# New places for all side jobs of a kernel generation, and a new order of its ring buffers, in a fused adaLN, S4 convolution and bilinear FFN kernel

## The chip, the cores and the metric

The kernel runs on one core of one Trainium2 chip. The metric is the device time in microseconds (us) of one execution; the times of a kernel are given as the median of its runs. A profiled execution is one further execution, seen instruction by instruction; its span runs from the first to the last instruction that the profile shows.

## What is computed

The inputs are a sequence `A_u` of 2048 rows of 640 channels, a condition vector `c`, and the weights. Cut to what matters:

```python
mod = (silu(c) @ w_mod).reshape(1, 6, 1, -1)          # sa, ca, ga, sb, cb, gb
h = layernorm(x) * (1 + ca) + sa
# S4: P[d,n,l] = exp(dt[d] * A[d,n] * l);  K[d,l] = Re sum_n C[d,n] P[d,n,l] dt[d] B[d,n]
y = irfft(rfft(pad(h)) * rfft(pad(K)))[:2048] + h * Dskip
x = x + ga * y
h = layernorm(x) * (1 + cb) + sb
x = x + gb * (((h @ w_gate) * (h @ w_up)) @ w_down)    # 640 -> 1536 -> 640
```

Length is 2048, there are 640 channels (five groups `db` of 128), 192 complex states per channel, and a hidden width of 1536. The time index l is split, so that exp(dt A l) is a product of short tables: tables are made, and their products are formed on the fly and multiplied on TensorE.

## The kernel before, in words

The program has two parts. The first generates the convolution kernel K and, beside that, does everything that the convolution needs; the second is the bilinear FFN, a long run of matmuls (L1059 and L1463) that the change leaves alone.

**The generation.** There are 40 blocks n (8 per channel group), each of three sub-steps, in the loop `for t in range(3*NK+24)`. A block passes through four engines. POOL (`kg_pool`, all at L710) forms three outer sums or products ahead of use: Ph (the angles of the next block), EQ and EP. ACT (L230) turns angles into sines, into PSUM tiles `tra` and `trb`. DVE multiplies the two: QtA and QtB (L765 to L767), PtA (L772), PtB (L792). PE contracts QtA with PtA (`kg_ma`, L807) and QtB with PtB (`kg_mb`, L822). EQ, EP, Ph, PtA and `tr` have two buffers each, so POOL forms EQ of block n+2 only after DVE's last QtB instruction (L767) of block n. Twice per channel group POOL also makes tables, `tab_ph` (L649, L650, L674, L693 to L695) and `tab_eq` (L674, L704, L705).

**The side jobs.** Everything else of the first part is cut into phases of Python generators, which `at` files under numbers and `due` lets go:

```python
        for v in ts:
            jobs.setdefault(v // 10, []).append((v, it))
...
        for _, g in sorted(jobs.pop(x, []), key=lambda j: j[0]):
            next(g, None)
```

In the loop, `due(2*t)` stands ahead of DVE's products of the sub-step and `due(2*t+1)` behind them and ahead of POOL's and PE's pieces. A block so has six steps; steps 0 to 239 lie in the generation, those below 0 ahead of it, and those from 240 on behind it. Within its engine each phase stands where its number puts it; engines take their instructions strictly in this order and wait by semaphores. The row of numbers is the dict `SCHED`. The jobs it places are:

- `mod_l`, `u_modr` (L360), `u_fold`, `u_modc`, `u_modg`: loads of `w_mod`, the six modulation rows, their folding.
- `u_stats`, `row_stats`, `u_hm`: loads of the rows of x, their layernorm, and its store to DRAM.
- `u_seeds(db)` (key `q`), 14 segments for each channel group after the first: loads, DVE arithmetic (L579 to L619, L644), and functions of ACT from three table sets, from which the tables of POOL come. The last segment (L644, L645) is what `tab_ph` of that group waits for.
- `e0`: ACT's exponentials for the second half of the first group, seven of LP, one of RH and one of RL, between two table loads.
- `u_k`, `u_pre`, `u_g`, `u_c` (L889; six adds on DVE, L930 to L936; inverse L946; store of WD), `u_d` (load TV from WD, matmul L967, add L971 or L974): the Fourier stages of K, of h and of their product.
- `rows`, `raw`, `split_g`, `u_head` (transposes L1139, matmuls L1176), `warm` (L1149; 30 and 4 matmuls into a tile that nobody reads): the beginning of the second part, at steps from 244 on.

**The buffers.** `ring(pool, shape, name)` gives a new tile the next letter of the string `SLOT[name]`, which decides the buffer, and so which earlier user it has to wait for:

```python
    def ring(pool, shape, name, dtype=F32):
        return pool.tile(shape, dtype, name=name + next(slot[name]), bufs=1)
```

The rings are the PSUM tiles psfa to psfc of the side jobs, and tiles in SBUF: gh, hf, TV, xs, Kt, W and f16.

Of the kernel before, what the change touches and what calls it, by code (L numbers as in the profile page):

```python
# [31 lines left out]
    ml=(-885, -929, -989),  # L32
    mr=(((98, 154), (90, 130)), ((-884, 78), (-877, 73)), ((-885, -881), (-889, 132))),
    st=(
        (-955, 11),
        (-929, 195),
        (-874, 149),
        (-925, 128),
        (-938, 121),
        (-879, 152),  # L40
        (-869, 167),
        (-924, 162),
        (-995, -925),
        (-938, -871),
        (-885, 93),
        (-990, -871),
        (50, 180),
        (51, 214),
        (-930, -878),
        (-927, 39),  # L50
    ),
    hm=(
        (120, 388),
        (119, 390),
        (123, 234),
        (-949, 306),
        (-1000, 254),
        (112, 246),
        (231, 293),
        (-871, 309),  # L60
        (266, 333),
        (324, 384),
        (315, 372),
        (134, 256),
        (463, 511),
        (335, 429),
        (391, 541),
        (479, 545),
    ),
    rstd=(228, 229),  # L70
    tab=(487, 829),
    fo=(157, 189, 197, 222),
    e0=(138,),
    ds=(205, 222, 503, 397),
    mc=((-872, 289, 307, 356, 356), (217, 378, 439, 446, 461), (309, 570, 620)),
    q=(
# [4 lines left out]
    ),  # L81
    pre=(
# [5 lines left out]
    ),  # L88
    c=(
# [56 lines left out]
    w=(2508, 2575, 2790, 2776, 2819, 2829),  # L146
# [1505 lines left out]
```

## Time and profile before

| what | value |
|---|---|
| median of 3 runs | 1003.26 us (1000.94 to 1003.36) |
| profiled execution, own time | 1001.29 us |
| its span | 999.2 us, so 2.09 us lie around it |
| TensorE clock granted, mean | 0.961 |
| busy: PE, DVE, POOL, ACT | 900.0, 762.8, 564.3, 561.9 us |
| generation on POOL | from 27.7 to 433.5 us |
| end of the first part on PE | 518.5 us |

The profile lists busy time by engine, groups of instructions with what ended the idle time before them, and the chain of work that ended last. In a group such as `EQ<-LQ,RH` the names are the tiles written and read; the line is that of the kernel or of a helper (L230 is the helper that records every ACT function, so there one goes by the tiles). A timeline row gives start, duration, engine, line, and in brackets the idle time before it with what ended that.

### The profile page before, as it was taken

The page shows a single profiled execution, that of the slowest core. Times are in us where ns is not written, and L with a number is a line of the kernel's source. Part 1 is how long each engine was busy: PE and PEld are TensorE (multiplying, and loading weights), DVE is VectorE, ACT ScalarE, POOL GpSimd, SP SyncE. Part 2 cuts the span into 40 slices and gives each one's busy share as a digit, 9 for nine tenths or more (in the row PEclk, how much of TensorE's full clock was granted, in tenths as well). Part 3 has the DMA queues.
Part 4 walks back from the last instruction along what each step waited for, and adds up shares of the span by engine and source line. Part 5 has one row for each costly group of instructions (what it writes and reads, how often), then busy time and mean ns, then how long its engine had stood idle before and what let it go on. Part 6 is the DMA issues. An engine that isn't in the chain of part 4 may idle for free.

```text
span 999.2 us, 26832 instructions
## 1 busy us (share of the span) xinstructions
PE 900.0 (90%) x11192; PEld 727.2 (73%) x11192; DVE 762.8 (76%) x1399; ACT 561.9 (56%) x1048; POOL 564.3 (56%) x415
## 2 busy tenths in 40 slices
PE   4867898899789689998888999999999999999998
PEld 3565556675576467776555888879998888889998
DVE  8798569889979997975769788777576887768452
ACT  4869989987878979752354323235463422223331
POOL 5978899799789899930032667650112365542000
PEclk9877889999899899999999999999999999999999
DMA  8728754555256454577673442535635232212341
GB/s 265 254 50 301 227 176 135 194 163 167 68 163 202 129 161 120 164 248 214 210 210 123 153 150 87 184 132 159 209 134 202 88 105 80 79 53 59 100 159 53
DMA packets 147817, 153.16 MB, mean 153 GB/s; under 512 B 9200, under 2 KB 125424, under 8 KB 146288
## 3 DMA queue, kind: packets, MB, share of 16 engines
q1 hardware_dynamic: 145968, 148.43, 46.8%
q10 hardware_dynamic: 1728, 3.02, 0.8%
q8 instruction: 88, 1.44, 0.6%
q14 instruction: 33, 0.27, 0.1%
HBM read 110.45 MB, written 40.96 MB: 152 GB/s over the span
## 4 chain that ended last, share of the span: by engine, by line
PE 63%; DVE 16%; ACT 10%; issue 4%; DMA 4%; POOL 2%; SPq 1%; DVEq 0%; ACTq 0%; POOLq 0%
PE pa L1059 26%; PE pa L1463 16%; PE kg L807 2%; DMA xsb<-A_u 2%; PE kg L822 2%; PE psfc L889 2%; ACT L230 1%; PE psfb L889 1%; PE psfa L889 1%; PE psfc L946 1%; PE psfb L946 1%; PE psfa L946 1%; PE psfc L868 1%; ACT trb L230 1%; PE psfa L844 1%
## 5 line engine op out<-in xcount | busy, mean ns | idle before, releaser
L710 POOL TENSOR_TENSOR EQ<-LQ,RH 128x1536 f32<-128x1536 f32 x40 | 124.2, 3105 | 9.9 <-DVE QtB L767 9.7
L230 ACT ACTIVATE z<-pa 128x512 f32<-128x512 f32 x24 | 14.4, 598 | 175.7 <-POOL a L1430 112.1
L1024 DVE TENSOR_TENSOR wsgl<-wga,wsgh 128x640 fp32r<-128x640 f32 x72 | 70.0, 976 | 46.1 <-ACT wsgh L230 46.1
L1412 POOL TENSOR_TENSOR z<-z,s 128x512 f32<-128x512 f32 x24 | 32.1, 1337 | 126.5 <-DVE s L1411 72.0
L230 ACT ACTIVATE wsgh<-wga 128x640 fp32r<-128x640 f32 x72 | 52.5, 732 | 65.1 <-PE pa L1463 47.9
L1024 DVE TENSOR_TENSOR wtl<-tf,wth 128x256 fp32r<-128x256 f32 (+1 forms) x72 | 42.7, 594 | 48.3 <-ACT wth L230 48.3
L1463 PE MATMUL pa<-wsgh,sh 128*128 128x384 f32 (+1 forms) x304 | 69.4, 309 | 0.0
L1463 PE MATMUL pa<-wsgh,sl 128*128 128x384 f32 (+1 forms) x304 | 69.0, 308 | 0.0
L1463 PE MATMUL pa<-wsgl,sh 128*128 128x384 f32 (+1 forms) x304 | 69.0, 308 | 0.0
L710 POOL TENSOR_TENSOR Phb<-LH,DH 128x1536 int32<-128x1536 int32 x20 | 62.3, 3115 | 11.2 <-ACT tra L230 11.2
L710 POOL TENSOR_TENSOR EP<-LP,RH 128x768 f32<-128x768 f32 x40 | 66.1, 1651 | 0.0
L710 POOL TENSOR_TENSOR Pha<-LH,DH 128x1536 int32<-128x1536 int32 (+1 forms) x21 | 62.5, 2974 | 2.2 <-ACT trb L230 1.9
L1036 POOL TENSOR_TENSOR tf<-wur,wgb 128x256 f32<-128x256 f32 x23 | 17.8, 776 | 75.6 <-DVE wtl L1024 50.0
L822 PE MATMUL kg<-QtB,PtB 64*32 64x64 f32 x2560 | 48.7, 229 | 5.4 <-DVE QtB L766 5.3
L822 PEld LDWEIGHTS kg<-QtB,PtB 64*32 64x32 f32 x2560 | 41.6, 114 | 15.4 <-issue 6.5
L1463 PEld LDWEIGHTS pa<-wsgh,sl 128*128 128x128 f32 x304 | 46.4, 187 | 0.0
L1463 PEld LDWEIGHTS pa<-wsgl,sh 128*128 128x128 f32 x304 | 46.3, 187 | 0.0
L1059 PE MATMUL pa<-sh,wtl 128*128 128x512 f32 x144 | 45.0, 394 | 1.4 <-DVE wtl L1024 1.2
L1463 PEld LDWEIGHTS pa<-wsgh,sh 128*128 128x128 f32 x304 | 46.3, 187 | 0.0
L1059 PE MATMUL pa<-sh,wth 128*128 128x512 f32 x144 | 44.9, 393 | 0.5 <-ACT wth L230 0.5
L1059 PE MATMUL pa<-sl,wth 128*128 128x512 f32 x144 | 44.5, 390 | 0.0
L1430 POOL TENSOR_TENSOR a<-s,z 128x512 f32<-128x512 f32 x24 | 38.8, 1618 | 5.4 <-DVE s L1429 5.4
(604 smaller groups left out, 2925.2 us busy)
## 6 DMA issues: line engine op xcount, KB each, us to landing
wga<-wdg SPq DMA_DIRECT2D x24, 640.0 KB, 5.0
wga<-B_w_gate SPq DMA_DIRECT2D x12, 640.0 KB, 5.9
wgb<-B_w_gate SPq DMA_DIRECT2D x24, 320.0 KB, 3.4
wur<-B_w_up SPq DMA_DIRECT2D x24, 320.0 KB, 4.0
xb<-x2d SPq DMA_DIRECT2D x6, 1280.0 KB, 5.7
TVb<-WD SPq DMA_DIRECT2D x22, 256.0 KB, 3.6
t_tw<-w_mod SPq DMA_DIRECT2D x3, 1600.0 KB, 8.5
t_ti<-w_mod SPq DMA_DIRECT2D x3, 1600.0 KB, 7.9
```

What stands on the lines that cost most here:

```text
L230: return S.activation(o, i, f, **kw)
L710: G.tensor_tensor(o.rearrange("p x (h l) -> p x h l", l=8), lo.unsqueeze(2).to_broadcast([P, rows, nh, 8]), hi.rearrange("p h x -> p x h") ...
L807: PE.matmul(kg[j * 32 : j * 32 + 32, dd, :], PtA[:, c, dl * 4 + j, :], QtA[:, c, dl * 4 + j, :], start=dd == 0 and c == 0, stop=False, til ...
L822: PE.matmul(kg[j * 32 : j * 32 + 32, dd, :], PtB[lo : lo + 64, c, r, :], QtB[lo : lo + 64, c, r, :], start=False, stop=dd == 7 and c == 1, ...
L889: PE.matmul(r[c][par * 64 : par * 64 + 64, i, :], t_tw[:, k0 + k, c, :], src[:, k, :], start=True, stop=True, tile_position=(0, par * 64))
L946: PE.matmul(r[par][:, i], t_ti[lo : lo + 64, qd * 4 + i, c, :], x[lo : lo + 64, c, i, :], start=c == 0, stop=c == 1, tile_position=(lo, 0))
L1024: V.tensor_tensor(lo, v, hi, op=OP.subtract)
L1036: E.tensor_tensor(t[:, 0:2], u[:, 0:2], g[:, 0:2], op=OP.subtract)
L1059: PE.matmul(ps, w[a][:, k], x[b][:, l], start=n == 0 and m == 0, stop=n == 2 and m == len(ks) - 1)
L1412: G.tensor_tensor(ZT[i], ZT[i], S67[i], op=OP.add)
L1430: G.tensor_tensor(a_tile(NF + i % NF), c, ZT.pop(i), op=OP.mult)
L1463: PE.matmul(ACC[tb][t][c], x[:, ts], w[:, cs], start=st, stop=f == NF - 1 and n == 2 and (c == 0 or t % 2 == 1))
```

## The change

Only numbers and letters change: the entries of `SCHED` and the strings in `SLOT`. Each engine executes the same instructions, but for ACT, which has 26 table loads in place of 24: a load is put in wherever a function needs another set than the one before it in ACT's order. The file gets five lines longer, so that a line of before stands five lines lower after the change.

```diff
 SCHED = dict(
-    ml=(-885, -929, -989),
-    mr=(((98, 154), (90, 130)), ((-884, 78), (-877, 73)), ((-885, -881), (-889, 132))),
+    ml=(-880, -938, -960),
+    mr=(((144, 184), (129, 179)), ((-877, 76), (-871, 133)), ((-890, -867), (-887, 14))),
...
-    rstd=(228, 229),
+    rstd=(180, 188),
...
-    e0=(138,),
+    e0=(29,),
...
-        (989, 1089, 1237, 1248, 1250, 1264, 1295, 1295, 1327, 1332, 1349, 1349, 1350, 1366),
+        (992, 1022, 1107, 1268, 1278, 1287, 1296, 1299, 1300, 1307, 1317, 1317, 1319, 1324),
...
-    w=(2508, 2575, 2790, 2776, 2819, 2829),
-    wl=(2444, 2450),
-    wm=(2801, 2834),
-    h=(2480, 2716, 2875, 2876, 2878, 2878, 2878, 2878),
+    w=(2574, 2477, 2623, 2825, 2760, 2598),
+    wl=(2501, 2487),
+    wm=(2775, 2703),
+    h=(2718, 2774, 2804, 2819, 2853, 2861, 2863, 2869),
```

The strings of the rings Ph, PtA, tr, W and f16 stay as they are; Kt, TV, gh, hf, psf and xs get others of the same length. What this does to the order of an engine is shown at three places.

**ACT, first blocks.** These are rows of before around `e0`, in block 2: two evictions of modulation rows (TVa, TVb), a table load, the exponentials, a load back, and the sines of the next sub-step.

```order
L230 ACTIVATE trb<-PtAa 128x512
L230 ACTIVATE TVa<-psfc 1x256
L230 ACTIVATE TVb<-psfb 1x256
L230 ACT_TABLE_LOAD
L230 ACTIVATE LP_146<-RL_156 128x96 x7
L230 ACTIVATE RH_153<-RH_153 128x1056
L230 ACTIVATE RL_156<-RL_156 128x288
L230 ACT_TABLE_LOAD
L230 ACTIVATE tra<-Pha 128x512
```

After the change the same rows stand in block 0, right behind the second pair of sines of that block:

```order
L235 ACTIVATE trb<-ab 128x512
L235 ACTIVATE TVb<-psfa 1x256
L235 ACTIVATE ab<-Pha 128x512
L235 ACTIVATE tra<-Pha 128x512
L235 ACTIVATE tra<-ab 128x512
L235 ACT_TABLE_LOAD
L235 ACTIVATE LP_146<-RL_156 128x96 x7
L235 ACTIVATE RH_153<-RH_153 128x1056
L235 ACTIVATE RL_156<-RL_156 128x288
L235 ACTIVATE ab<-Pha 128x512
L235 ACT_TABLE_LOAD
L235 ACTIVATE trb<-Pha 128x512
```

The exponentials and their two loads have moved by eleven steps, ahead of the last sines of block 0 (`trb<-Pha`, which POOL's third Ph waits for).

**DVE, the seeds of the fourth channel group.** Rows of before in block 22, between QtB of block 21 and PtAa of block 22: QtA of block 22, the six adds of `u_c`, and the first row of the segment with the reciprocal.

```order
L767 SCALAR_TENSOR_TENSOR QtB<-tra,EQ_141 128x8x32
L601 TENSOR_SCALAR psfb<-ptb 128x192
L765 TENSOR_TENSOR QtA<-trb,EQ_140 128x32x32
L766 TENSOR_TENSOR QtA<-trb,EQ_140 128x16x32
L767 SCALAR_TENSOR_TENSOR QtA<-trb,EQ_140 128x16x32
L930 TENSOR_TENSOR TVb<-psfc,ghb 128x512
L931 TENSOR_TENSOR TVb<-psfc,ghb 128x512
L932 TENSOR_TENSOR psfc<-psfa,ghb 128x512
L933 TENSOR_TENSOR psfa<-psfa,ghb 128x512
L935 TENSOR_TENSOR TVb<-TVb,psfc 128x512
L936 TENSOR_TENSOR TVb<-TVb,psfa 128x512
L614 SCALAR_TENSOR_TENSOR prm<-ptb,dt_98,psfb 128x192
```

After the change the reciprocal's segment stands right behind QtB of block 21, then the six adds, and from these on the row goes:

```order
L940 TENSOR_TENSOR TVa<-TVa,psfa 128x512
L941 TENSOR_TENSOR TVa<-TVa,psfb 128x512
L649 COPY RL_155<-psfc 128x96
L649 COPY RL_156<-psfc 128x96
L650 TENSOR_SCALAR ptb<-psfc 128x192
L770 TENSOR_TENSOR QtA<-trb,EQ_140 128x32x32
L771 TENSOR_TENSOR QtA<-trb,EQ_140 128x16x32
L772 SCALAR_TENSOR_TENSOR QtA<-trb,EQ_140 128x16x32
L777 TENSOR_TENSOR PtAa<-tra,EP_142 128x1024
```

The last segment of the seeds (L649, L650; before L644, L645) now stands ahead of QtA and PtAa of block 22; before it stood behind both.

**PE, the end of the first part.** Rows of before from the last pieces on: `u_d` (L967), the 34 warm matmuls (L1149), the transposes (L1139) and products (L1176) of the head.

```order
L967 MATMUL psfb<-TVb,ct 32x512 x4
L1149 MATMUL psg<-wsgh 128x512 x34
L967 MATMUL psfc<-TVa,ct 32x512 x4
L967 MATMUL psfa<-TVb,ct 32x512 x4
L1139 MATMUL psfb<-ident,hfa 128x128 x4
L1139 MATMUL psfc<-ident,hfb 128x128 x4
L967 MATMUL psfa<-TVa,ct 32x512 x4
L1139 MATMUL psfb<-ident,hfc 128x128 x4
L1176 MATMUL psg<-hh_6985,wsgh 128x512
```

After the change:

```order
L972 MATMUL psfa<-TVa,ct 32x512 x4
L1154 MATMUL psg<-wsgh 128x512 x30
L972 MATMUL psfb<-TVb,ct 32x512 x4
L972 MATMUL psfc<-TVa,ct 32x512 x4
L972 MATMUL psfa<-TVb,ct 32x512 x4
L1144 MATMUL psfb<-ident,hfc 128x128 x4
L1144 MATMUL psfc<-ident,hfa 128x128 x4
L972 MATMUL psfa<-TVa,ct 32x512 x4
L1144 MATMUL psfb<-ident,hfb 128x128 x4
L1181 MATMUL psg<-hh_7302,wsgh 128x512
```

Four of the warm matmuls have gone ahead of the last inverse; the third `u_d` behind the warm ones (of channel group 4, quarter 2) stands ahead of the head's first transposes, and a fourth follows (group 0, quarter 2). Before, that fourth one and the `u_d` of group 4, quarter 3, came as the very last pieces of the first part; after, the latter stands between two products of the head.

More of the change, by code (lines that the diff above doesn't have):

```diff
@@ new lines @@
+    hm=(
+        (350, 404),
+        (197, 446),
+        (63, 188),
+        (-948, 283),
+        (-866, 201),
+        (2, 196),
+        (193, 237),
+        (-895, 316),
+        (253, 338),
+        (338, 365),
+        (264, 341),
+        (38, 228),
+        (354, 517),
+        (365, 462),
+        (472, 540),
+        (517, 565),
+    ),
+    rstd=(180, 188),
+    tab=(644, 765),
+    fo=(200, 212, 246, 268),
+    e0=(29,),
+    ds=(386, 334, 572, 308),
+    mc=((-869, 234, 279, 323, 374), (225, 501, 521, 567, 581), (346, 429, 486)),
```

162 lines of the change are left out of this document (74 added, 88 removed), and 45 rows, old and new, of tables (c, d, g, pre).

## The prediction

> **What bounds the kernel now.** I read the page's totals first, then busy time by stretch, then the groups of the engine that paces the first part, then what it waits for. The totals, and the engines' shares of the chain that ended last:
>
> ```profile
> PE 900.0 (90%) x11192; PEld 727.2 (73%) x11192; DVE 762.8 (76%) x1399; ACT 561.9 (56%) x1048; POOL 564.3 (56%) x415
> PE 63%; DVE 16%; ACT 10%; issue 4%; DMA 4%; POOL 2%; SPq 1%; DVEq 0%; ACTq 0%; POOLq 0%
> ```
>
> PE looks like the bound everywhere, but that is an average over two parts. By stretch (columns: length, then busy us of PE, PEld, DVE, ACT and POOL with counts, the granted clock, DMA share, GB/s):
>
> ```profile
> 300.00:434.00 134.00, 116.08 (x2902) 86.59 (x2898) 119.85 (x195) 111.87 (x204) 128.41 (x74) 0.96 0.53 157
> 434.00:545.00 111.00, 94.36 (x1136) 67.34 (x1134) 78.90 (x190) 48.19 (x90) 10.68 (x16) 0.98 0.66 203
> 545.00:999.00 454.00, 446.74 (x2378) 395.27 (x2376) 316.82 (x506) 157.27 (x305) 169.35 (x152) 1.00 0.38 122
> ```
>
> From 545 us on PE is busy 446.7 of 454.0 us with work that the change does not touch; whatever is gained or lost before shifts this part as a whole. From 300 to 434 us POOL is the fullest, 128.4 of 134.0 us: in the generation POOL sets the pace, and all others have gaps. Its three pieces of a block:
>
> ```profile
> L710 POOL TENSOR_TENSOR EQ<-LQ,RH 128x1536 f32<-128x1536 f32 x40 | 124.2, 3105 | 9.9 <-DVE QtB L767 9.7
> L710 POOL TENSOR_TENSOR Phb<-LH,DH 128x1536 int32<-128x1536 int32 x20 | 62.3, 3115 | 11.2 <-ACT tra L230 11.2
> L710 POOL TENSOR_TENSOR EP<-LP,RH 128x768 f32<-128x768 f32 x40 | 66.1, 1651 | 0.0
> ```
>
> A block costs POOL 3.11 + 3.12 + 1.65 = 7.9 us, and no number of the change alters that. So a side job moved on ACT, DVE or PE is free as long as POOL does not come to wait for it; the price of this change is the change in POOL's waits, plus what comes after POOL's last block (about 434 us). The waits (line, releaser, us in total, times, longest):
>
> ```profile
> POOL Phb L710 <- ACT tra L230: 11.2, 4, 5.0
> POOL DL L650 <- issue: 11.2, 2, 7.5
> POOL EQ L710 <- DVE QtB L767: 9.7, 3, 6.2
> ```
>
> Some 32 us at nine places, and these are all that re-placing can win before the tail. I go through the places where the order changes beside POOL.
>
> **1. ACT's exponentials in block 0.** Rows of PE, ACT and POOL at the start and in block 2:
>
> ```profile
> 18.50 4.64 PE L360 MATMUL psfb<-t_tw,sil 128*128 128x256 f32 x10
> 22.93 3.44 PE L360 MATMUL psfa<-t_tw,sil 128*128 128x384 f32 x10
> ...
> 26.40 0.48 ACT L230 ACTIVATE TVa<-psfa 1x384 f32<-1x384 f32 x1 [9.10 <-PE psfa L360]
> 30.03 0.63 ACT L230 ACTIVATE ab<-Pha 128x512 f32<-128x512 int32 x1
> 33.12 0.60 ACT L230 ACTIVATE trb<-ab 128x512 f32<-128x512 f32 x1
> 44.38 1.28 ACT L230 ACT_TABLE_LOAD   x1
> 48.33 1.28 ACT L230 ACT_TABLE_LOAD   x1
> 49.62 0.60 ACT L230 ACTIVATE tra<-Pha 128x512 f32<-128x512 int32 x1
> ...
> 35.46 3.10 POOL L710 TENSOR_TENSOR Pha<-LH,DH 128x1536 int32<-128x1536 int32 x1
> ```
>
> The moved stretch, load to load, lasts 49.62 - 44.38 = 5.2 us. It now stands ahead of the sines that end at 33.12 + 0.60 = 33.7 us, and POOL's third Ph (35.46 us) needs their tile. Against that, PE now forms the row 1x384 first (3.44 us instead of 4.64 + 3.44 for both), so ACT's first eviction can come some 3 to 4 us before 26.40; but the second eviction, which the new order puts between the sines of block 0, still waits until both are formed, about 26.4 us, so only the first sines gain. Behind it stand 3.7 us of sines (30.03 to 33.72 in the old order) and the 5.2 us: the last sines end at about 26.9 + 3.7 + 5.2 = 35.8 us. POOL waits half a us there, and one or two more if the load of `w_mod`, which stands behind two more loads of x on SP, lands later. In return ACT is 5.2 us freer in block 2, where DVE's longest backlog of the start arose (the 6.2 us in the third row of the waits, at 69 us). DVE's work from block 0 to 5 is the same set of pieces in a changed order, and its end releases the tables of the next group. I book 0, with ends of -3 and +5.2 (the whole stretch, if nothing pays it back).
>
> **2. Two more table loads.** Each is one row of 1.28 us, and the next function starts 49.62 - 48.33 = 1.29 us after the load's start: 2.6 us more on ACT, both in the seeds of groups 2 and 3. ACT is not the pacer there as a whole; the one that stands in the path goes into item 4. [...]
>
> **3. Groups of six adds in blocks 16 to 19.** `u_c` gives DVE a group of six adds. Rows: DVE's products of a half block, one such group by its first and last add, and a lead of DVE over POOL two blocks on:
>
> ```profile
> 262.80 0.69 DVE L792 TENSOR_TENSOR PtB<-tra,EP 128x512 f32<-128x512 f32 x1
> 264.33 0.42 DVE L767 SCALAR_TENSOR_TENSOR QtB<-tra,EQ 128x256 f32<-128x256 f32 x1
> 265.23 1.22 DVE L765 TENSOR_TENSOR QtA<-trb,EQ 128x1024 f32<-128x1024 f32 x1
> 266.95 0.68 DVE L767 SCALAR_TENSOR_TENSOR QtA<-trb,EQ 128x512 f32<-128x512 f32 x1
> 267.61 0.69 DVE L930 TENSOR_TENSOR TVb<-psfc,ghb 128x512 f32<-128x512 f32 x1
> 270.81 0.68 DVE L936 TENSOR_TENSOR TVb<-TVb,psfa 128x512 f32<-128x512 f32 x1
> 275.07 1.23 DVE L772 TENSOR_TENSOR PtAa<-tra,EP 128x1024 f32<-128x1024 f32 x1 [0.29 <-ACT tra L230]
> 276.98 0.35 DVE L645 TENSOR_SCALAR ptb<-psfb 128x192 int32<-128x192 f32 x1
> ...
> 203.94 0.41 DVE L767 SCALAR_TENSOR_TENSOR QtB<-tra,EQ 128x256 f32<-128x256 f32 x1
> ...
> 209.48 3.11 POOL L710 TENSOR_TENSOR EQ<-LQ,RH 128x1536 f32<-128x1536 f32 x1
> ```
>
> A block of products is 1.95 (262.80 to 264.75) + 2.40 + 1.23 = 5.6 us, the six adds 270.81 + 0.68 - 267.61 = 3.9 us: together 9.5 us, 1.6 more than POOL's block. The steps of these groups were 93, 106, 114, 120 (blocks 15, 17, 19, 20) and become 96, 104, 113, 118 (blocks 16 to 19 without a pause). Three such blocks cost 4.8 us of lead before POOL's own tables, which move to block 19, give time back; the lead was 209.48 - 204.35 = 5.1 us. It just holds: +0.5, ends 0 and +3 (two seed segments come into these blocks as well; one of the same kind lay between 271.49 and 275.07 above, 3.6 us, which bounds them).
>
> **4. The seeds of group 3 (block 22 to 21).** POOL's rows at that place:
>
> ```profile
> 264.89 3.11 POOL L710 TENSOR_TENSOR EQ<-LQ,RH 128x1536 f32<-128x1536 f32 x1 [2.30 <-DVE QtB L767]
> 277.46 0.39 POOL L650 TENSOR_TENSOR DL<-ptb 128x96 int32<-128x96 int32 x1 [7.51 <-issue]
> ```
>
> The 7.51 us are the largest wait of the generation: the tables need the DVE row that ends at 276.98 + 0.35 = 277.33 us. That row now comes ahead of QtA (2.40) and PtAa (1.23), 3.6 us sooner; an add of 0.7 us comes in before it, and on ACT's side of the same path one table load more (1.28). That leaves -3.6 + 0.7 + 1.3 = -1.6, and I book -1.8 with the 0.2 us idle ahead of 264.96. QtB of block 21 comes 1 to 2 us later, as that add and the row L601 now stand ahead of it, but what POOL then waits there it doesn't wait at the tables: this is inside the wait and not added. Ends: -5 (DVE reaches the place with less backlog, since fewer adds stand in blocks 20 to 23) and +1. The whole wait, 9.8 us, cannot go, as the chain of DVE remains.
>
> **5. The seeds of group 4 (block 29).** Before, one wait:
>
> ```profile
> 349.42 3.12 POOL L710 TENSOR_TENSOR Phb<-LH,DH 128x1536 int32<-128x1536 int32 x1 [3.96 <-ACT tra L230]
> ```
>
> The exponentials move ahead of two sines, which changes only which of them wait; the sum of ACT's pieces ahead of this Ph is the same. Two evictions of `u_c` (0.6 us each, as the rows of 128x512 on ACT) come ahead of the arctangent whose result the tables of group 4 need; where they find no gap they cost 1.2 us. I take +0.8, with ends 0 and the 3.96 us that a sine waits there once more.
>
> **6. The tail.** The end of the first part, from the chain, and PE's rows there:
>
> ```profile
> 485.24 7.95 PE psg L1149 x34
> 515.84 0.99 PE psfb L967 x8
> 518.51 1.53 PE pa L1139 x12
> ...
> 498.71 0.86 PE L1139 MATMUL psfb<-ident,hfa 128*128 128x128 f32 x4 [2.92 <-ACT hfa L230]
> 500.98 2.61 PE L967 MATMUL psfa<-TVa,ct 64*32 64x512 f32 x8 [0.56 <-DMA TVa<-WD]
> ...
> L1024 DVE TENSOR_TENSOR wsgl<-wga,wsgh 128x640 fp32r<-128x640 f32 x72 | 70.0, 976 | 46.1 <-ACT wsgh L230 46.1
> ```
>
> The two last `u_d` leave the end: 518.51 - 515.84 = -2.7 us, and they find room in PE's gaps of 2.92 us and the like. Four of the 34 warm matmuls (7.95 us) leave the stretch in which PE waits for WD anyway: 0 to -0.9, the load lands when it lands. Against it the head's first transposes (498.71) now stand behind the `u_d` whose TV arrives at 500.98: its loads stand ahead of two stores in SP's row now and come some 3 us sooner, an estimate, so that its 2.61 us end at about 500.6, +1.9 (+4.9, if they come no sooner); a `split_g` inside the head adds one DVE row (0.98 us mean), and one transpose tile now shares its PSUM buffer with the one before, 1 to 2 us that DVE's later release costs, of which the head's own waits hide the half. The last store of WD is queued behind an eviction more, up to +1.2. Sum about -0.5; ends -3 and +3.
>
> **The sum.** 0 + 0.5 - 1.8 + 0.8 - 0.5 = -1.0 us, on 1001.29 us of the profiled execution. That one lies 2.0 us under the median of the runs, within their spread of 2.4 us; the same step from the median gives 1003.26 - 1.0 = 1002.3 us. Within 0.3% (3 us) a measurement of this kernel can hardly tell a time from no change. The forecast is no change that can be seen.
>
> **Rivals.** (a) Slower: the start is not paid back. ACT's stretch of 5.2 us ahead of block 0's sines delays POOL, and DVE, which is behind from block 2 to 5 anyway, ends as much later. This decides from the point at which what POOL waits more at 36 us is not taken off its later waits for QtB, the longest of which is 6.2 us. For it: the modulation rows' load stands later in SP's row; against it: ACT and DVE have the same sum of work up to block 5. Time: 1002.3 + 5.2 = 1007.5 us. (b) Faster: DVE comes to the seeds of group 3 without a backlog, so that the tables start when the end -5 of item 4 says, and the tail keeps its 2.7 us: 1002.3 - 3.2 - 2.2 = 996.9 us. For it: before, DVE's groups of adds stood in blocks 19, 20, 22 and 23, now one fewer lies close ahead; against it: the backlog that leaves there enters blocks 16 to 18. [...] By rows alone, (c) is that a load falls into a sine's path in both places, 2.6 us.
>
> **How the numbers follow.** Forecast 0.34, (a) 0.33, (b) 0.30, (c) 0.03. Of the forecast's 0.34, 0.24 lie within 3 us of the median, 0.06 under and 0.04 over; (b) is all faster, (a) and (c) are slower but for 0.02. So faster 0.36, same 0.26, slower 0.38: both signs hold most of the chance. The forecast's own range, from independent ends, is 998 to 1007. The wide range takes in (b) with its further end (two favourable ends more, -4) and (a) with one unfavourable end more (+4): 993 to 1012.
>
> **What would show it.** Item 1: POOL's third Ph waits up to 2 us at about 36 us, and the wait for QtB of 6.2 us at 69 us shrinks by as much. Item 3: no wait for QtB over 2 us between 190 and 260 us. Item 4: the wait before L650 near 277 us shrinks from 7.51 to 4 or 5 us, with one for QtB of some 3 or 4 us ahead of it. Item 6: the second part starts 0 to 3 us after POOL's end plus 84.5 us (518.5 - 434). Wrong it would be if POOL's last block ended elsewhere than at 429 to 439 us, or if DMA landings, which I took as before, moved by microseconds.

## The result, and the profile after

The changed kernel takes 1031.96 us, median of 4 runs (1026.2 to 1033.94), against 1002.1 us before on the same chip (996.91 to 1003.36): ratio 1.0299, 95% interval [1.0241, 1.0356]. It is 30 us slower; the forecast was 1002.3 us and no visible change, the range 993 to 1012 us. The profiled execution took 1030.6 us, its span 1028.7 us. Totals and shares of the chain, from its page:

```profile
PE 912.9 (89%) x11192; PEld 733.9 (71%) x11192; DVE 770.5 (75%) x1399; ACT 563.7 (55%) x1050; POOL 564.7 (55%) x415
PE 62%; DVE 12%; ACT 9%; DMA 7%; issue 4%; POOL 4%; SPq 1%; DVEq 0%; ACTq 0%; POOLq 0%
```

These hardly differ from before; nobody reads 30 us out of them. The second part, in a stretch of 453 us where 454 were shown of before, is the same (446.55 busy us of PE against 446.74):

```profile
575.00:1028.00 453.00, 446.55 (x2378) 395.71 (x2378) 317.25 (x507) 157.32 (x305) 169.28 (x152) 1.00 0.38 122
```

So the loss lies in the first part. POOL's work there is unchanged too (EQ 124.1 us, before 124.2). What grew are its waits:

```profile
POOL Phb L715 <- ACT tra L235: 29.3, 7, 7.9
POOL EQ L715 <- DVE QtB L772: 16.0, 8, 5.1
POOL DL L655 <- issue: 10.3, 3, 4.8
POOL Pha L715 <- ACT trb L235: 7.6, 4, 2.8
POOL LQ L709 <- DVE RL L649: 4.1, 1, 4.1
```

Waits for ACT's sines went from 11.2 to 29.3 us (Phb) and from 1.9 to 7.6 us (Pha), waits for QtB from 9.7 to 16.0. With the waits ahead of POOL's tables (11.2 us before at L650, now 10.3 at L655 and 4.1 at L709) that is 34.0 us before and 67.3 after: 33.3 us more, which is POOL's lateness at the end of the generation, 33.8 us.

**Where.** POOL forms one EQ per block, so the end of each can be laid beside that of before: the lateness of EQ n, counted from 0 (EQ 39 ended at 431.9 us before). In us, for the changed kernel in two profiles (the second belongs to the last experiment):

| EQ | 2 | 8 | 14 | 16 | 19 | 23 | 24 | 28 | 33 | 36 | 39 |
|---|---|---|---|---|---|---|---|---|---|---|---|
| changed | 2.4 | 8.5 | 8.3 | 17.1 | 19.1 | 21.9 | 17.5 | 20.2 | 24.4 | 33.8 | 33.8 |
| changed again | 2.1 | 10.4 | 11.5 | 20.6 | 23.8 | 26.7 | 23.2 | 25.6 | 29.6 | 33.1 | 34.7 |

This table is the best reading of the case: lateness comes in a few jumps, stays flat between them, and falls for good only once, at EQ 24. There is one at EQ 7 and 8 (+6), one at EQ 15 and 16 (+9), one at EQ 34 to 36 (+9.3 in one profile, +3.5 in the other), and some of 2 to 4 us. The tail gives 2.8 us back, for the second part starts 549.44 - 518.51 = 30.9 us later:

```profile
549.44 2.18 PE pa L1144 x20
```

### The profile page after: what moved, and what is told of

Read it like the earlier page. It is cut to its first block, busy times and chain, and to the rows that moved or that the text cites. A ratio compares the mean times of both kernels' runs of the same rounds, so it can differ in the third digit from the quotient of the medians.

```text
span 1028.7 us, 26822 instructions
## 1 busy us (share of the span) xinstructions
PE 912.9 (89%) x11192; PEld 733.9 (71%) x11192; DVE 770.5 (75%) x1399; ACT 563.7 (55%) x1050; POOL 564.7 (55%) x415
## 4 chain that ended last, share of the span: by engine, by line
PE 62%; DVE 12%; ACT 9%; DMA 7%; issue 4%; POOL 4%; SPq 1%; DVEq 0%; ACTq 0%; POOLq 0%
PE pa L1064 25%; PE pa L1468 16%; PE psfa L894 2%; PE kg L812 2%; PE kg L827 2%; PE psfb L894 2%; DMA hm<-gha 2%; PE psfb L873 2%; PE psfb L951 1%; PE psfc L894 1%; ACT trb L235 1%; PE psfa L873 1%; POOL EQ L715 1%; DMA TVa<-WD 1%; PE psfa L951 1%
## 5 line engine op out<-in xcount | busy, mean ns | idle before, releaser
L715 POOL TENSOR_TENSOR EQ<-LQ,RH 128x1536 f32<-128x1536 f32 x40 | 124.1, 3104 | 16.4 <-DVE QtB L772 16.0
L715 POOL TENSOR_TENSOR Phb<-LH,DH 128x1536 int32<-128x1536 int32 x20 | 62.3, 3113 | 29.3 <-ACT tra L235 29.3
```

The source lines that it names most:

```text
L715: G.tensor_tensor(o.rearrange("p x (h l) -> p x h l", l=8), lo.unsqueeze(2).to_broadcast([P, rows, nh, 8]), hi.rearrange("p h x -> p x h") ...
```

## The experiments

Theory A: the loss is a sum of local stalls, none of which is given back. Rivals: it has no single place (B), later slack pays it back (C, in the first four runs), each stall taken away turns up elsewhere (D). Later came theory F (evictions stand too soon behind their matmuls) and the clock theory, which the texts on record also call C, with rival G against it. Where a mixed table brings jobs into another order, the rings' letters had to follow. Each experiment's rows carry its own kernel's line numbers, so one function has several in what follows.

### Parts of the change alone

Start only (keys `ml, mr, st, hm, rstd, tab, fo, e0, ds, mc` and `q[0]` from the changed kernel, the rest from before), and then all jobs up to about step 110:

```diff
 start_only:   + ml mr st hm rstd tab fo e0 ds mc q[0] low[.][0]
 to_step_110:  + the same, and pre[0] pre[1] g[0] c[0] k[0:16] q[1] low[.][1:3]
```

> Kernel: the kernel before, with only the start of the new table (modulation, statistics, rows of hm, folding, the late exponentials, the twiddle tables, seeds of channel block 1, the first pair of small tables); everything from the first FFT input on keeps its old place. Theory A (the loss is a sum of local stalls, each of which stays): in the changed kernel's trace POOL is 8.2 to 8.3 us late once the start is over (steps 38 to 81), so this kernel is 8 us slower than before, with POOL late by about 6 us at its fourteenth Phb. Rival B (no single place: the loss comes from the two halves together, or from the letters of the rings): under 3 us. Rival C (a late POOL gives the rest slack, which is given back later): the trace shows 8 us at step 40, the end only 0 to 4 us.

> Kernel: the start as in the kernel with the start only, and also the FFT work of channel block 0, the FFT inputs of block 1, the first eight and second eight pieces of the generated kernel, and the seeds of block 2 at their new places (steps 0 to about 110); the rest as before. Theory A: POOL was 17.1 us late at step 91 and 19.0 us at step 109 of the changed kernel, so 17 to 19 us slower than before. Rival B: under 6 us. Rival C: 17 us at step 100, the end 5 to 12 us.

The other part, and of that the later FFT jobs alone:

```diff
 from_step_110: + all that to_step_110 leaves at its old place
 late_fft_only: + pre[3:5] g[2:5] c[2:5] d[2:5] k[24:40] low[.][7:9] w wl wm h
```

> Kernel: the other part of the change alone: start, block 0 and seeds of block 2 as before, all later jobs (FFT work of blocks 1 to 4, seeds of blocks 3 and 4, later small tables, the head of the second part) at their new places. Theory A: what is left of the changed kernel's loss, 33.8 - 19.0 = 14.8 us on POOL at the end of the generation, less 2.8 us won in the tail, so 12 us slower than before; item 4 of the prediction is in it with -1.6 us, item 5 with +3.6 us. Rival B: under 5 us. Rival C would make it the full 28 us less what the first part gave.

> Kernel: before, with the FFT work of blocks 2 to 4 from their spectra on, the FFT inputs of blocks 3 and 4, the last sixteen kernel pieces, the last pair of small tables and the head at their new places; the seeds of blocks 3 and 4 stay at their old ones. Theory A: the stall at steps 195 to 205 (+10 us on POOL) comes with it and the tail gives 2.8 us back, so 6 to 8 us slower than before. If that stall needs the seeds of block 4 at their new place as well: -3 to +1 us. Rival B: within 2 us.

Against before: 1.0285 [1.0243, 1.0326], 1.0367 [1.0307, 1.0427], 1.0258 [1.0181, 1.0335] and 1.0236 [1.0185, 1.0287]. All four missed their expected times, and the two halves together lose far more than the whole. The lateness says why:

| EQ | 2 | 8 | 10 | 14 | 16 | 19 | 23 | 24 | 33 | 36 | 39 |
|---|---|---|---|---|---|---|---|---|---|---|---|
| start only | 0.5 | 9.5 | 14.9 | 24.5 | 25.5 | 25.5 | 26.8 | 26.8 | 28.6 | 28.6 | 28.6 |
| to step 110 | 1.7 | 9.5 | 9.5 | 10.3 | 16.1 | 28.3 | 31.8 | 31.7 | 34.1 | 34.1 | 34.1 |
| from step 110 | 0.0 | -2.3 | -2.3 | -2.3 | -1.1 | 8.8 | 16.8 | 13.4 | 20.1 | 30.9 | 31.0 |
| late FFT only | 0.1 | -1.8 | -1.8 | -1.8 | -1.9 | -1.9 | -1.0 | 9.1 | 19.3 | 25.6 | 25.6 |

Where a mixed kernel carries new places, it has the jumps of the changed one: +9.5 up to EQ 8 with the start, about +6 at EQ 16 with block 0, +11 and +6 at EQ 34 to 36 with the late FFT jobs, the +6 in the kernel without the new seeds of block 4. Where it has old places it is flat: the start-only kernel goes through the last 25 blocks 24.5 us late and adds 4.1 us, so rival C is out. But every joint of the two tables makes a jump of its own, 9 to 15 us at EQ 9 to 11, 19 or 24, so B's "no single place" holds for the whole time: a half of a table fits nowhere but beside its own other half. The -2.3 us at EQ 8 of a kernel in which nothing had moved there say what chance does between two profiles: some 2 us.

### One entry at a time

In the changed kernel, single entries were moved to where a wait had been seen:

```diff
 row9_later:     -hm[9]=(338, 365)              +hm[9]=(338, 395)
 input13_later:  -pre[1][3]=(796, 816, 827)     +pre[1][3]=(796, 876, 886)
 input42_later:  -pre[4][2]=(1942, 1971, 1992)  +pre[4][2]=(1942, 2052, 2065)
 three_later:    all three
```

> Kernel: the changed kernel with one entry altered: the normalisation of row group 9 of hm (second phase of u_hm(9)) stands at step 39 instead of 36; no ring letter changes. Theory A (at step 37 ACT stood 6.63 us in front of that row's reload, which waited for a store of the same ring buffer, which waited behind the 1600 KB load of modulation weights, and the sines stood behind it): POOL's step of +5.9 us at its eighth EQ is gone or down to 1 us, and the kernel is 5 us (3 to 6) faster than the changed one, 1026 to 1028 on the clock of its own runs. Rival D (a stall of that size moves on to the next tight place, as the joints of the mixed kernels each cost 9 to 15 us): within 2 us of the changed kernel.

> Kernel: the changed kernel with the second and third phase of u_pre(1,3) at 876 and 886 instead of 816 and 827, so that its matmuls no longer stand right behind those of u_c(0,1) and ask for PSUM buffers that the six products of u_c(0,1) still read; the rings' letters follow from there. Theory A: POOL's +8.8 us between its EQ 14 and EQ 16 falls to 0 to 4 us, and the kernel is 5 to 9 us faster than the changed one. Rival D: the input's new place stalls something as long: within 2 us. Rival E (the delay there is the exponentials of block 2, which stand 7.8 us on ACT, and not the ring): within 2 us, and POOL's wait at that block for the sines stays at 6 us.

> Kernel: the changed kernel with the second and third phase of u_pre(4,2) at 2052 and 2065 instead of 1971 and 1992, where it stood right behind the matmuls of u_c(2,3); the rings' letters follow. Theory A: POOL's +10 us between its EQ 33 and Ph 36 falls to 0 to 4 us, and the kernel is 6 to 10 us faster than the changed one. Rival D: within 2 us.

> Kernel: the three edits together. Theory A: they are at three places on one line of work, and their gains add: 16 to 24 us faster than the changed kernel, POOL 10 to 16 us late at the end of the generation instead of 33.8, so 6 to 14 us slower than before. Rival D: 0 to 8 us faster than the changed kernel.

Against before: 1.0282 [1.0227, 1.0337], 1.0305 [1.0243, 1.0368], 1.0292 [1.0243, 1.0342], 1.0304 [1.0253, 1.0355]: none differs from the changed kernel. Row group 9 was the wrong one, ACT stood in front of row group 8, and the jump at EQ 7 stayed. With input (1,3) later the jump from EQ 14 to 16 fell from 8.8 to 3.7 us, and with all three to 4.8, as theory A has it, but from EQ 16 to 19 came 8.5 us instead of 1.9, as rival D has it. Rival E has something too: POOL's wait for the sines behind the exponentials was 5.08 us with the input moved, 6.09 in the changed kernel, and 5.03 before, so that wait is not the input's, and the change made it only 1.1 us longer. For input (4,2) nothing can be said: the jump from EQ 33 to 36 was 5.2 and 2.6 us with it moved, but in kernels where that stretch was not edited it was 9.3, 9.3, 3.5, 3.5 and 3.6 us. That it has two sizes became the question of the last runs.

### The load of the modulation weights

SP's row of the changed kernel, and what ACT stood for (start, length, engine, line, transfer; in brackets the idle time):

```profile
76.89 0.50 SPq L358 DMA_DIRECT2D t_tw<-w_mod  x1
77.44 4.01 SPq L490 DMA_DIRECT2D hm<-gha  x1
...
94.42 0.33 SPq L470 DMA_DIRECT2D gha<-A_u  x1
```

```profile
77.44 16.96 DMA hm<-gha
94.42 2.77 DMA gha<-A_u
...
97.28 0.92 ACT gha L235
98.19 0.52 ACT ab L235
```

```profile
97.28 0.92 ACT L235 ACTIVATE gha<-gha,nm,rs 128x640 f32<-128x640 f32 x1 [6.63 <-DMA gha<-A_u]
99.34 3.11 POOL L715 TENSOR_TENSOR Phb<-LH,DH 128x1536 int32<-128x1536 int32 x1 [7.87 <-ACT tra L235]
```

A store of a row group goes out right behind the 1600 KB load of `w_mod` and lands 16.96 us later; the reload of its buffer waits for that; ACT, in order, waits 6.63 us for the reload, the sines stand behind it, and POOL waits 7.87 us for those.

```diff
 weights_later: -mc[1][0]=225  +mc[1][0]=270
```

> Kernel: the changed kernel with one entry altered: the 1600 KB load of the modulation weights for block row 4 (first phase of u_modc(4)) goes out at step 27 instead of 22, behind the stores of row groups 11 and 6 and the reloads of 8 and 10; no ring letter changes. The kernel with row group 9 later had moved a row that nobody waited for: ACT stood in front of row groups 8 and 10 there. Theory A (their reload waits for a store of the same buffer, and the store for the weights in front of it): POOL's step of 6 to 8 us at its eighth EQ falls to 0 to 2 us, and the kernel is 4 to 7 us faster than the changed one. Rival D (such a gain is lost again at the next tight place): the step at EQ 7 goes, but POOL is within 2 us of the changed kernel at EQ 39.

```profile
76.81 0.50 SPq L378 DMA_DIRECT2D hm<-gha  x1
77.36 0.42 SPq L378 DMA_DIRECT2D hm<-ghb  x1
89.59 0.33 SPq L358 DMA_DIRECT2D gha<-A_u  x1
90.27 0.35 SPq L358 DMA_DIRECT2D ghb<-A_u  x1
90.71 0.39 SPq L246 DMA_DIRECT2D t_tw<-w_mod  x1
```

```profile
92.82 0.92 ACT L123 ACTIVATE gha<-gha,nm,rs 128x640 f32<-128x640 f32 x1 [1.47 <-DMA gha<-A_u]
94.89 3.10 POOL L603 TENSOR_TENSOR Phb<-LH,DH 128x1536 int32<-128x1536 int32 x1 [3.50 <-ACT tra L123]
```

The reload goes out 4.8 us sooner, ACT's wait falls from 6.63 to 1.47 us, POOL's from 7.87 to 3.50, and POOL is 4.1 us late at EQ 8, not 8.5 or 10.4. So the load is shown to make 4 to 6 us of that jump of 6 to 8, and what is gained there is kept (19.5 us at EQ 33 against 24.4 and 29.6). It is not the whole of the store's 16.96 us: with no load in front, the reload still goes out 12.8 us behind the store (76.81 to 89.59). The step at EQ 7 by itself fell only to 4.4 us, where 0 to 2 were expected; it is EQ 8 that gives the rest. The whole time, 1.0276 [1.0226, 1.0326], cannot be told from the changed kernel's by itself.

### Evictions later

```diff
 evictions_later, e.g.: -g[0][0]=(648, 781, 793)   +g[0][0]=(648, 781, 803)
                        -c[0][0]=(..., 892, 892)   +c[0][0]=(..., 892, 903)   14 entries
```

> Kernel: the changed kernel with 14 evictions of side matmuls (last phases of u_pre(2,0), (2,3), (4,0), of u_g(0,0), (0,2), (1,2), (2,3), (3,1) and fourth phases of u_c(0,0), (0,1), (2,1), (2,2), (3,1), (3,3)) moved by 5 to 23 places, just far enough that ACT does a pair of sines of the generation between their matmuls and them; no ring letter changes. Theory F (ACT comes to an eviction before TensorE has done its matmuls, waits 2 to 4 us there, and the sines that POOL needs stand behind): ACT's idle time in front of evictions of hf, W and gh, 27.4 + 17.5 + 8.1 us in the changed kernel against 8.9 + 6.3 + 4.7 before, falls by 15 to 30 us, and the kernel is 8 to 20 us faster than the changed one. Rival D: the waits go elsewhere, within 3 us of the changed kernel.

Theory F fell: 1.0461 [1.0407, 1.0515], and 48.6 us late at EQ 39. ACT's idle time in front of the evictions hardly fell (hf 31.4, W 7.0, gh 5.8 us). One reason may be that an eviction is also what gives the PSUM buffer back, so that TensorE waits longer for a late one. Here are TensorE and ACT in that kernel, around the jump of EQ 15 and 16:

```profile
184.93 0.44 PE L782 MATMUL psfa<-f16b,t_tw 128*64 128x128 f32 x4 [1.77 <-ACT gha L123]
191.53 0.44 PE L782 MATMUL psfa<-f16b,t_tw 128*64 128x128 f32 x4 [1.73 <-DVE TVa L828]
198.02 1.08 PE L761 MATMUL psfa<-hfc,ct 64*64 64x512 f32 x1 [2.99 <-issue]
```

```profile
202.60 0.60 ACT L123 ACTIVATE hfa<-psfa 128x512 f32<-128x512 f32 x1 [7.71 <-PE psfb L761]
```

At the same places the changed kernel has 0.63, 1.53, 3.15 and 5.85 us. So TensorE waits 1.1 us more for the eviction of gha here, and ACT 1.9 us more at the next one; what made the rest of the 14.8 us was not taken apart.

### One stall made in the kernel before, and two edits at the other end

```diff
 input42_early_in_before: -pre[4][2]=(1908, 2085, 2090)  +pre[4][2]=(1890, 1922, 1934)
 input42_and_g23_later:   -pre[4][2]=(1942, 1971, 1992)  +pre[4][2]=(1942, 2052, 2065)
                          -g[2][3]=(1880, 1945, 1952)    +g[2][3]=(1880, 1945, 1963)
```

> Kernel: the kernel before with one job moved: u_pre(4,2) at 1890, 1922 and 1934 instead of 1908, 2085 and 2090, so that its matmuls stand right behind those of u_c(2,3) and the six products, as in the changed kernel; the rings' letters follow. Theory A (that neighbourhood alone makes a stall): POOL 3 to 6 us late from its Ph 34 on and to the end, so 3 to 6 us slower than before. Rival (it needs the other jobs around it as well): within 2 us.

> Kernel: the changed kernel with u_pre(4,2) later as in the kernel tried before (2052 and 2065) and the eviction of u_g(2,3) at 1963 instead of 1952, behind a pair of sines. With the first alone POOL's wait of 4.07 us for its Phb was gone, those of 2.78 us (Pha) and 2.37 us (EQ) stayed. Theory F: they go too, POOL's step from EQ 33 to Ph 36 falls from 9.3 us to 0 to 3 us, and the kernel is 6 to 9 us faster than the changed one. Rival D: other waits of 4 us and more take their place.

One job moved in the kernel before makes it slower, 1.0059 [1.0033, 1.0086]; POOL is 2.0 us late by it at EQ 36, 2.2 at the end, less than expected, the rest of the 5.8 us lies behind POOL's last block. The second kernel lost: 1.0352 [1.0316, 1.0389], with 5.0 us from EQ 33 to 36 and more everywhere ahead of that, where it carries the changed kernel's places and buffers (12.8 us late at EQ 14, against 8.3 and 11.5): chance, as far as can be told. Theory F's 0 to 3 us for that step were missed.

### The clock

The same instructions, in the two profiles of the changed kernel, at u_pre(4,2). First profile, then second (the second column is the length of one matmul; L812 is the generation's next):

```profile
410.86 0.92 PE L873 MATMUL psfb<-hfc,ct 64*64 64x512 f32 x1 [2.43 <-issue]
411.03 1.11 PE L873 MATMUL psfc<-hfc,ct 64*64 64x512 f32 x1
...
414.85 1.94 PE L812 MATMUL kg<-QtA,PtAa 128*32 128x64 f32 x64
```

```profile
413.42 0.61 PE L873 MATMUL psfb<-hfc,ct 64*64 64x512 f32 x1 [2.44 <-issue]
415.62 1.10 PE L812 MATMUL kg<-QtA,PtAa 128*32 128x64 f32 x64
```

The pause is the same, 2.43 and 2.44 us; in one the clock is halved behind it (1.11 us for a matmul, 1.94 for the group; granted 0.89 from 385 to 425 us), in the other it is not (0.61, 1.10; granted 1.00). POOL's jump from EQ 33 to 36 is 9.3 us in the first and 3.5 us in the second. The three other kernels in which that stretch was not edited go the same way: where the first matmul behind the pause is already slow (1.02 us, input (1,3) later) the jump is 9.3 us, where it takes 0.61 (row group 9 later, weights later; granted 0.96 from 385 to 425 us in both) it is 3.5 and 3.6. That is five profiles in step, but no test. To test it, zeros were added to an open accumulator, first all over the generation:

```diff
+    def keep(m):
+        PE.matmul(kg_of[m][:, 0:4, :], ident, zero.unsqueeze(2).to_broadcast([P, 4, 64]), start=False, stop=False)
+        if 3 <= t <= 3 * NK and t % 6 in (3, 4, 5, 0):
+            keep((t - 3) // 6)
+        if t < 3 * NK and t % 6 in (2, 3, 4, 5):
+            keep((t - 2) // 6)
```

> Kernel: the changed kernel with some 160 additional matmuls, each of which adds zeros (256 columns) to an open accumulator of the generation, after the side jobs and at the end of the steps in which one is open; nothing else moves. Theory C (TensorE's pauses of 2 to 3 us halve its clock, and that is a good part of each stall: the same pause of 2.4 us behind u_c(2,3) cost POOL 9.8 us where the clock fell in it, and 3.6 us where it did not): the granted clock between 27 and 432 us rises from 0.85 to above 0.90 and POOL is 8 to 18 us less late at EQ 39 than in the changed kernel. Rival G (the clock only follows the pauses): the clock rises, POOL stays within 4 us of 33.8 us, or is later, since the matmuls themselves (0.3 to 0.4 us each) stand in TensorE's row.

> Kernel: the kernel before with the same additional matmuls. Under theory C the clock, 0.91 there between 27 and 432 us, has little to win: POOL within 4 us of the kernel before at EQ 39. It says what the added matmuls cost by themselves; the difference of the two kernels with them is what is left of the change at a held clock, 15 to 22 us by theory C, 30 us or more by rival G.

1.0589 [1.0539, 1.0639] and 1.0369 [1.0346, 1.0392]. The clock rose (27 to 432 us: from 0.86 to 0.93, and from 0.91 to 0.95), but POOL was 54.9 and 33.7 us late, so both expectations of POOL missed: TensorE's row has no room for the 160 calls. Before, TensorE idled 61 of the 405 us (PE busy 344 us), and 160 calls of some 0.48 us (the six below take 2.88) come to 77. The difference of the two, 21.2 us, lies in theory C's bracket, but with so large a cost of their own it decides nothing. So only the two pauses were filled:

```diff
+    FILL[1, 3] = lambda: keep(6, 6, False)      # six ahead of u_pre(1,3)
+    FILL[4, 2] = lambda: keep(15, 5, True)      # five ahead of u_pre(4,2)
 def u_pre(db, q):
+        if (db, q) in FILL:
+            FILL[db, q]()
         r = [ring(PF[-1], [P, 4, P], "psf") for _ in range(2)]
```

> Kernel: the changed kernel with eleven zero matmuls (256 columns, about 0.4 us each) in TensorE's own pauses, six ahead of the matmuls of u_pre(1,3), where it stood 3.15 us, and five ahead of those of u_pre(4,2), where it stood 2.43 us. They end before the PSUM buffers that it waits for are free, so nothing starts later by them. Theory C (a part of these stalls is the clock that falls in the pause): POOL's step from EQ 33 to EQ 36 is 3 to 5 us, not 9.3 to 9.9, and the one from EQ 14 to EQ 16 falls from 8.8 to 4 to 6 us; the kernel is 3 to 9 us faster than the changed one. Rival G (the clock only follows): both steps as before, 8 to 9 us, and 4 or 9 to 10 us.

> Kernel: the changed kernel with the eleven zero matmuls once more, for a second profile, since the step that they act on had two sizes without them. Theory C: again 3 to 5 us from EQ 33 to EQ 36. Rival G: 4 or 9 to 10 us by chance.

> Kernel: the same eleven matmuls in the kernel with the load of the modulation weights later. Theory C: the two gains add, POOL 14 to 20 us late at EQ 39, where the load alone gave 24.8; 10 to 16 us faster than the changed kernel. Rival G: 24 us or more.

> Kernel: the changed kernel as it is, for a second profile. Both theories: POOL's steps up to EQ 33 as in the first profile, within 2 us; the step from EQ 33 to EQ 36 either 4 or 9 to 10 us, as in the kernels in which that stretch was not edited.

On one chip: changed kernel 1033.54 us (1027.92 to 1036.63), pauses filled 1022.35 (1021.71 to 1026.01) and 1023.59 (1021.81 to 1027.02), with the weights later as well 1017.99 (1012.55 to 1021.47), before 1002.62. Against before that is 1.0305 [1.0261, 1.0349], 1.0207 [1.0173, 1.0242], 1.0222 [1.018, 1.0264] and 1.0151 [1.0107, 1.0196]. Eleven matmul calls, six that add zeros and five that write them into a buffer not yet in use, make the kernel some 10.6 us faster, a little more than the 3 to 9 us expected. The load later on top gives 5.0 us more: the slowest of its four runs, 1021.47 us, lies just under the fastest of the eight without it. That slowest one is the profiled one, so POOL's 20.9 us at EQ 39 (14 to 20 expected) shows little of it. The first pause, in the changed kernel and then filled (each call has two rows in the trace, so x12 are the six):

```profile
182.09 0.39 PE L894 MATMUL psfb<-f16b,t_tw 128*64 128x128 f32 x4
...
185.79 0.70 PE L894 MATMUL psfa<-f16b,t_tw 128*64 128x128 f32 x4 [1.53 <-DVE TVa L940]
...
188.54 0.67 PE L894 MATMUL psfa<-f16b,t_tw 128*64 128x128 f32 x4
188.97 0.50 PE L894 MATMUL psfb<-f16b,t_tw 128*64 128x128 f32 x4
192.62 1.08 PE L873 MATMUL psfa<-hfc,ct 64*64 64x512 f32 x1 [3.15 <-issue]
...
197.09 1.93 PE L812 MATMUL kg<-QtA,PtAb 128*32 128x64 f32 x64
```

```profile
188.57 0.69 PE L897 MATMUL psfa<-f16b,t_tw 128*64 128x128 f32 x4 [1.09 <-DVE TVa L943]
...
191.74 0.40 PE L897 MATMUL psfb<-f16b,t_tw 128*64 128x128 f32 x4
192.07 2.88 PE L1288 MATMUL kg<-zero,ident 128*128 128x256 f32 x12
195.33 1.04 PE L876 MATMUL psfa<-hfc,ct 64*64 64x512 f32 x2 [0.39 <-issue]
...
198.01 1.10 PE L812 MATMUL kg<-QtA,PtAb 128*32 128x64 f32 x64
```

From the first matmul of u_pre(1,3) to the generation's group is 4.47 us in the one and 2.68 in the other, and the group itself takes 1.10 us, not 1.93. The pause of 3.15 us is not where the slow clock begins: the matmuls ahead of it are slow in both kernels (0.67 to 0.70 us, not 0.39), behind a pause of 1.53 and of 1.09 us. In both the clock comes back at the end of that run; with the zeros it then stays, without them it is at half again behind the pause. In the second profile of the changed kernel the clock of this stretch is as low as in the first: 0.70 and 0.71 from 180 to 215 us.

What POOL waited at this jump, changed and then filled:

```profile
190.87 3.10 POOL L715 TENSOR_TENSOR Phb<-LH,DH 128x1536 int32<-128x1536 int32 x1 [6.09 <-ACT tra L235]
198.42 3.10 POOL L715 TENSOR_TENSOR EQ<-LQ,RH 128x1536 f32<-128x1536 f32 x1 [4.45 <-DVE QtB L772]
208.28 0.39 POOL L655 TENSOR_TENSOR DL<-ptb 128x96 int32<-128x96 int32 x1 [4.82 <-issue]
```

```profile
193.64 3.10 POOL L715 TENSOR_TENSOR Phb<-LH,DH 128x1536 int32<-128x1536 int32 x1 [6.95 <-ACT tra L235]
201.14 3.10 POOL L715 TENSOR_TENSOR EQ<-LQ,RH 128x1536 f32<-128x1536 f32 x1 [4.40 <-DVE QtB L772]
206.28 0.39 POOL L655 TENSOR_TENSOR DL<-ptb 128x96 int32<-128x96 int32 x1
```

So the jump has two halves. The first, 4.3 us up to EQ 15 (5.2 filled), stays: the sines behind the exponentials, and QtB, ahead of which the six adds of `u_c(0,1)` and the reciprocal's segment stand on DVE (189.25 to 196.42 us); before, these two waits were 5.03 and 1.16 us. The second, 4.5 us at EQ 16, is the wait for the tables of the third channel group, whose matmuls stand behind u_pre(1,3) on TensorE; this one goes with the slow clock.

The stretches of before, changed again and pauses filled (the third number from the end is the granted clock):

```profile
180.00:215.00 35.00, 32.57 (x778) 24.26 (x780) 28.47 (x47) 30.32 (x54) 31.69 (x23) 1.00 0.55 177
```

```profile
180.00:215.00 35.00, 29.33 (x518) 19.31 (x514) 23.78 (x41) 24.34 (x49) 19.17 (x15) 0.70 0.40 131
```

```profile
180.00:215.00 35.00, 31.87 (x640) 22.78 (x630) 28.87 (x49) 30.35 (x61) 23.18 (x20) 0.95 0.54 175
```

| EQ | 8 | 14 | 16 | 19 | 24 | 33 | 36 | 39 |
|---|---|---|---|---|---|---|---|---|
| changed again | 10.4 | 11.5 | 20.6 | 23.8 | 23.2 | 29.6 | 33.1 | 34.7 |
| pauses filled | 9.6 | 10.2 | 15.1 | 15.1 | 13.4 | 18.6 | 20.6 | 21.6 |
| filled again | 10.6 | 11.4 | 15.3 | 15.3 | 13.6 | 18.9 | 20.8 | 23.5 |
| weights later, filled | 5.2 | 5.9 | 9.1 | 9.0 | 7.4 | 14.2 | 20.4 | 20.9 |

From EQ 14 to 19 the changed kernel loses 12.3 us (10.8 in the first profile), the filled one 4.9 and 3.9. From EQ 33 to 36 the filled kernel loses 2.0 and 2.0 us, less than the 3 to 5 expected. The second profile of the changed kernel kept each step up to EQ 33 within 2 us of the first, as expected, but they add up to 5.2 us at EQ 33. That a halved clock carries a good part of these stalls is shown for the first; for the second its size was 3.5 or 9.3 without and 2.0 with, but 6.2 us in the kernel with the weights later, at full clock (that group took 1.10 us there too), so a jump of that size comes without the clock too: there ACT stood 2.51 and 2.20 us for TensorE ahead of two evictions, and POOL waited 2.91 us for the sines and 2.33 us for QtB.

## Why the prediction was wrong

**Item 1 (0, ends -3 and +5.2).** The third Ph waited 2.33 us, as said:

```profile
37.88 3.12 POOL L715 TENSOR_TENSOR Pha<-LH,DH 128x1536 int32<-128x1536 int32 x1 [2.33 <-ACT trb L235]
```

POOL is 2.3 us late by it at EQ 6: inside the ends. The payback in block 2 did not come: the wait for QtB of 6.2 us went, but in its place POOL waits 6.79 us for the sines one piece earlier (75.01 us). Rival (a) had this mechanism at 5.2 us, and the right sign, but not the loss.

**Item 2.** No loss at a table load was seen at either place: the loads are rows of 1.28 us after the change too, POOL has no wait from 116 to 184 us, around the one that is new in the seeds of group 2 (167.20 us), and waits for no sine from 242 to 300 us, around those of group 3. Rival (c), a load in a sine's path in both places, is not supported.

**Item 3 (+0.5).** From EQ 17 to 19 POOL lost 1.9 us, inside the ends, but with the pause filled it lost nothing there (15.1 us at EQ 16 and at EQ 19), so this is the slow clock's and not the adds'. The sign named, "no wait for QtB over 2 us between 190 and 260 us", failed at EQ 15 (4.45 us), though not through the six adds alone (above).

**Item 4 (-1.8).** Right in mechanism and size:

```profile
286.79 3.08 POOL L715 TENSOR_TENSOR EQ<-LQ,RH 128x1536 f32<-128x1536 f32 x1 [5.09 <-DVE QtB L772]
...
295.00 0.39 POOL L655 TENSOR_TENSOR DL<-ptb 128x96 int32<-128x96 int32 x1 [3.17 <-issue]
```

The wait of 7.51 us became 3.17, with one for QtB ahead of it (5.09 us, more than the 3 or 4 named); from EQ 22 (19.4) to 24 (17.5) that nets -1.9 us, and -1.0 in the second profile.

**Item 5 (+0.8, ends 0 and +4).** From EQ 28 to 33 it cost 4.2 us, just past the upper end, and not by the one longer wait for a sine that this end stood for: POOL waited four times, 2.12, 2.33, 0.86 and 2.32 us (QtB, sines, QtB, tables). **Item 6 (-0.5, end -3).** The tail won 2.8 us, near its lower end; its terms were not taken apart.

These sum to 2.3 + 1.9 - 1.9 + 4.2 - 2.8 = +3.7 us. The other 27 us lie at places that the prediction did not look at. The step that failed is in the sum: it has six items, "the places where the order changes beside POOL", and puts POOL's new waits anywhere else at nothing, without a reason. The bound it rests on, "Some 32 us at nine places, and these are all that re-placing can win before the tail", holds for a gain only. Re-placing can win only what is waited, but it can lose anywhere; here POOL's waits grew by 33.3 us. Three such places were:

- EQ 7 and 8, +6.2 us: the store and the load of `w_mod` in SP's row. The prediction's last line said that DMA landings moving by microseconds would make it wrong; it took them as before instead of reading who stood behind 1600 KB in the new row. Shown, by the run with that load later, for some 4 of the 6 us.
- EQ 15 to 19, 11 to 12 us with item 3's 1.9 in it: u_pre(1,3) stands right behind u_c(0,1), whose six products still read the buffers that it asks for. TensorE stands 3.15 us, runs at half clock behind that, and ACT stands 5.85 us at the evictions ahead of the sines (4.00 with the pause filled). Two thirds of it, 8 us of 12, go when the pause is filled; the other 4 to 5 us, POOL's waits at EQ 15, do not. Moving the job alone makes the jump smaller and another one behind it.
- EQ 34 to 36, 3.5 or 9.3 us: the same pattern at u_pre(4,2), with and without a halved clock. How much the clock has in it stays open, as single profiles range over 2 to 6 us here.

The granted clock itself stood in the rows that the prediction quoted (0.96, 0.98, 1.00) and was used nowhere: the clock of before was taken as a property of the kernel, not as something the order had to keep up (from 27 to 432 us it was 0.91 before and 0.86 after).

Of the 30.9 us on the last chip, 10.6 go with the two filled pauses and 5.0 more with the load; 15.4 us are left. That remainder, several jumps of 2 to 5 us, was not taken apart, so the cause of half the loss stays open; nor did any run change the rings' letters alone. Rival (b) did not occur.

## What to carry to other kernels

When a tuned order is replaced as a whole, its slack is not a number that can be kept on account: each neighbourhood of jobs had been fitted, and keeping a part of the tuned order kept little of its time: the four mixtures were 2.4 to 3.7% slower than it, the whole new order 3.0%. Look at the places where the pacing engine did not wait, and ask of each what stands in front of it now, in the queue of transfers and in each engine that works in order. Where TensorE comes to stand in a stretch that it shares with other engines, read the granted clock there (slow matmuls followed a pause of 1.09 us here, and did not follow one of 2.44 us). Here eleven spare matmuls in two pauses were worth 10.6 us; moving the two jobs behind these pauses brought no gain that the times show (1.0305 and 1.0292, the changed kernel 1.0299).

## What the runs showed of the hardware

- A pause of 3.15 us on TensorE was followed by half the clock (granted 0.50 from 193 to 198 us; L812 1.93 us, not 1.10), one of 1.53 us too (L894 0.67 us, not 0.39), and so was one of 1.09 us in the kernel with the pauses filled (L897 0.67 us). One of 2.43 us was followed by it in one profile, and one of 2.44 us at the same place in another profile of the same kernel was not. Half the clock lasted from 185.8 to 189.2 us behind the 1.53 us, and from 192.6 to 209.6 us behind the 3.15 us, though TensorE was busy for all but 0.02 of these 17.0 us. What decides when the clock falls and when it comes back was not shown.
- Two profiles of one kernel differed by 6 us at the one place where the clock fell in only one of them (9.3 and 3.5 us). Its times differ by 0.8% (1026.2 to 1033.94 us in one set of runs); that the clock makes this too was not shown.
- 160 matmul calls on zeros, spread over the generation, made POOL 33.7 us late in the kernel before, though the granted clock rose from 0.91 to 0.95; eleven, in two pauses, made the changed kernel 10.6 us faster.
- A store of 320 KB that went out right behind a load of 1600 KB on the same queue landed after 16.96 us; with that load moved behind it, the reload that waits for it went out after 12.8 us.
